# Attention decode layer, forward and backward: the products of a pair moved behind the next pair's maximum, and the depth of the K and V loads changed

## The chip, the cores and the metric

The kernel runs on one core of a Trainium2 chip. The metric is device time in microseconds (us) of one execution. Three runs of the kernel before took 1701.25, 1701.69 and 1703.4 us, a median of 1701.69 us.

## The reference

One layer for decoding, with its gradients: a layer norm, attention of one new token per batch entry over a cache of 4096 keys (4 batch entries, 32 heads, head size 128), a residual, a second layer norm, a SwiGLU block, and then the vector-Jacobian product with a given output gradient. There are 128 (batch, head) pairs, called heads below; K and V of one head are 1024 KB each in bf16. The reference, cut to what matters:

```python
q = (layernorm(x) @ wq).reshape(B, 1, H, Dh).transpose(0, 2, 1, 3)
scores = einsum("bhqd,bhkd->bhqk", q, k_cache) * Dh**-0.5
p = softmax(scores)                               # over 4096 keys
o = einsum("bhqk,bhkd->bhqd", p, v_cache)
h = x + o.transpose(0, 2, 1, 3).reshape(B, 1, H * Dh) @ wo
out = h + swiglu(layernorm(h), w1, w3, w2)
# outputs: out, and the gradients for grad_out of x, k_cache, v_cache, wq, wo, w1, w3, w2
```

The gradients of the two caches are 128 MB each, and they are written out in full. Every head's K is read once and its V twice, once in the forward part and once in the backward part.

## The kernel before

The forward part goes over the heads in 64 pairs. For a pair it transposes K, multiplies by the query (S), takes the softmax, and then forms for each head PK, the keys scaled by their probabilities, on VectorE (DVE). One run of matrix products of V with PK gives M for a head, a 128 x 128 matrix from which the backward part takes the gradient of the query without reading K again; a last column of it is the head's output. The iterations overlap: in iteration gi the pair a = 2 gi, a + 1 goes through the softmax, the next pair's K (na, nb) is transposed, and M of the heads m1 = a - 3 and m2 = a - 2 is made.

All large buffers are slots that hold one head (or as much of something else), 23 in all. A slot that is given back goes to the end of a queue of free slots, and a load takes the one at its head; the load then waits until the last reader of what lay in that slot is done. All loads are issued by one engine (SyncE, SP), in the order of the program. M of 16 heads takes one slot for good, so the slots in use by M grow from one to eight in the forward part.

The parts that matter, cut where marked by `...`:

```python
G, VQ, NSLOT, NPE = 2, 3, 23, 1      # heads in a pair, V heads ahead, slots, head chunks transposed on TensorE
# NH = 128 heads, NGI = 64 pairs, MC = 16 heads in one M slot, SJ = 32 key chunks of a head, Dh = P = 128

    free = deque(range(NSLOT))

    class Slot:
        def __init__(self, name, src=free):
            self.i = src.popleft()
            self.t = slotp.tile([P, SLOT], BF16, name=name, tag=f"slot{self.i}")

        ...
        def heads(self):
            return self.t[:, 0:SJ * Dh].rearrange("p (j d) -> p j d", d=Dh)

        def give(self):
            free.append(self.i)

    def load_K(s):
        if s < NH:
            Ks[s] = Slot("Kn")
            nc.sync.dma_start(out=Ks[s].heads(), in_=cache_head(A_k_cache, s))

    def load_V(s):
        if s < NH and s >= nvl["n"]:
            nvl["n"] = s + 1
            Vs[s] = Slot("Vn")
            nc.sync.dma_start(out=Vs[s].heads(), in_=cache_head(A_v_cache, s))

    def more_K(s):
        while len(Ks) + kdone["n"] < min(NH, s + 8) and len(free) > 1:
            load_K(len(Ks) + kdone["n"])

    def T_pe(s):
        KTs[s] = Slot("KT")
        KT, Kn = KTs[s].heads(), Ks[s].heads()
        for c in range(NPE):
            pt = psT.tile([P, GW, P], BF16, tag="tps", name="pt_tps")
            for i in range(GW):
                nc.tensor.transpose(pt[:, i, :], Kn[:, c * GW + i, :], ident_b[:])
            nc.scalar.copy(out=KT[:, c * GW:(c + 1) * GW, :], in_=pt[:])

    def T_dve(s, c, n=1):
        KT, Kn = KTs[s].b().bitcast(FP32), Ks[s].b().bitcast(FP32)
        w_ = GW * Dh // 2
        nc.vector.transpose(out=KT[:, c * w_:(c + n) * w_], in_=Kn[:, c * w_:(c + n) * w_])

    def q_stationaries(gi): ...     # GpSimd: the query columns of a pair, W and zq

    def S_head(gi, hl):             # TensorE: 16 score products of one head, then its KT slot is free
        ...
        KTs.pop(s).give()

    # softmax of a pair, one step each:
    # sm_max    DVE   mx <- S_ps (max over the free dim), mxm <- mx
    # sm_max_T  PE    x_ps <- transpose of mxm
    # sm_gmax   DVE   gm <- x_ps
    # sm_bcast  PE    b_ps <- gm
    # sm_exp    DVE   nm <- b_ps;  ACT  E <- exp(S_ps, nm), row sums
    # sm_sum    PE    l_ps <- row sums
    # sm_norm   DVE   rl <- l_ps;  ACT  Pn <- E, rl
    # sm_P      PE    pt_P <- 8 transposes of Pn;  ACT  P_all <- pt_P (4 copies)

    def PK_pairs(s):
        PKs[s] = Slot("PK")
        PK = PKs[s].t[:].rearrange("p (j c) -> p j c", c=PKW)
        nc.gpsimd.tensor_copy(out=PK[:, :, Dh:PKW], in_=P_all[:, s, :, None].to_broadcast([P, SJ, 2]))

    def PK_mul(s):
        PK = PKs[s].t[:].rearrange("p (j c) -> p j c", c=PKW)
        nc.vector.tensor_tensor(
            out=PK[:, :, 0:Dh].rearrange("p j (r t) -> p j r t", t=2),
            in0=Ks[s].heads().rearrange("p j (r t) -> p j r t", t=2),
            in1=PK[:, :, None, Dh:PKW].to_broadcast([P, SJ, Dh // 2, 2]),
            op=ALU.mult,
        )
        Ks.pop(s).give()
        kdone["n"] += 1

    def M_mm(s, j0, j1):
        if j0 == 0:
            hold["M"] = psM.tile([P, PKW], FP32, name="M_ps", tag="M")
        PK = PKs[s].t[:].rearrange("p (j c) -> p j c", c=PKW)
        Vn = Vs[s].heads()
        for j in range(j0, j1):
            nc.tensor.matmul(hold["M"][:], lhsT=Vn[:, j, :], rhs=PK[:, j, :], start=(j == 0), stop=(j == SJ - 1))

    def M_end(s):
        w = s % 32
        PK = PKs[s].t[:].rearrange("p (j c) -> p j c", c=PKW)
        if w == 0:
            hold["kP"] = psK.tile([P, 4, Dh], FP32, name="kP_ps", tag="kP")
        for c in range(2):
            for q in range(4):
                j0 = (c * 4 + q) * 4
                nc.tensor.matmul(hold["kP"][32 * q:32 * (q + 1), :, :], lhsT=ones_window(w), rhs=PK[:, j0:j0 + 4, 0:Dh],
                                 start=(w == 0 and c == 0), stop=(w == 31 and c == 1), tile_position=(0, 32 * q))
        if s % MC == 0:
            Ms.append(Slot("M"))
        nc.scalar.copy(out=M_of(s), in_=hold["M"][:, 0:Dh + 1])
        PKs.pop(s).give()
        Vs.pop(s).give()

    def kP_flush(s): ...            # once in 32 heads: the key sums, out of PSUM and onto columns (takes a slot and gives it back)
    def O_cols(s0, s1): ...         # once in 16 heads: two small DVE copies

    for gi in range(NGI):
        nxt = gi < NGI - 1
        a, na, nb = gi * G, gi * G + 2, gi * G + 3
        m1, m2 = a - 3, a - 2
        pk1 = a - 1
        has1, has2, hasp = 0 <= m1 < NH, 0 <= m2 < NH, 0 <= pk1 < NH
        S_head(gi, 0)
        S_head(gi, 1)
        weights(gi)
        if has1:
            M_mm(m1, 0, 16)
        sm_max(gi)
        if nxt:
            q_stationaries(gi + 1)
            T_pe(na)
            T_dve(na, 1)
        sm_max_T(gi)
        if has1:
            M_mm(m1, 16, SJ)
        sm_gmax(gi)
        sm_bcast(gi)
        if nxt:
            T_dve(na, 2)
        sm_exp(gi)
        if has1:
            M_end(m1)
            load_V(m1 + VQ)
            if m1 % 32 == 31:
                kP_flush(m1)
            if m1 % MC == MC - 1 and m1 < NH - 1:
                O_cols(m1 - MC + 1, m1 + 1)
        if hasp:
            PK_pairs(pk1)
        if nxt:
            T_dve(na, 3)
            T_pe(nb)
            T_dve(nb, 1)
        sm_sum(gi)
        sm_norm(gi)
        if gi == NGI - 1:

            nc.scalar.sqrt(warm[:], warm[:])
        if hasp:
            PK_mul(pk1)
            more_K(pk1 + 1)
        weights(gi)
        if has2:
            M_mm(m2, 0, 24)
        sm_P(gi)
        if has2:
            M_mm(m2, 24, SJ)
            M_end(m2)
            load_V(m2 + VQ)
        weights(gi)
        PK_pairs(a)
        if nxt:
            T_dve(nb, 2, 2)
        PK_mul(a)
        more_K(a + 1)
        weights(gi)
        hold.pop(gi - 3, None)
        if 2 <= gi:
            step("d")

    # after the loop: products and M of the last heads, the attention output, layer norm, the MLP forward and
    # its gradient, then the first output gradient (grad_V(0)); in this part wo, w1, w3 and nine heads of V are loaded ahead
    # backward, per head: V transposed on TensorE, dP, and on VectorE the outer products gv and gk, 1024 KB out each
    ...
```

Of the kernel before, what the change touches and what calls it, by code (L numbers as in the profile page):

```python
# [13 lines left out]
AX = mybir.AxisListType  # L14

G = 2
VQ = 3
SLOT = 4160
NSLOT = 23
JQ = 8  # L20
# [4 lines left out]
def kernel(  # L25
# [22 lines left out]
    nc = tc.nc  # L48
# [6 lines left out]
    Dh = A_k_cache.shape[3]  # L55
    F = B_w1.shape[1]
    NH = B * H
# [4 lines left out]
    SJ = Sk // P  # L62
# [4 lines left out]
    MC = 16  # L67
# [83 lines left out]


    def more_K(s):
        while len(Ks) + kdone["n"] < min(NH, s + 8) and len(free) > 1:
            load_K(len(Ks) + kdone["n"])

    kdone = {"n": 0}
# [152 lines left out]
    hold = {}  # L310
# [5 lines left out]
# [13 lines that stand above are left out]
# [29 lines left out]
    def sm_max(gi):  # L358
        st = hold[gi]
        mx = fw.tile([P, 1], FP32, tag="mx", name="mx")  # L360
        nc.vector.tensor_reduce(out=mx[:], in_=st["S"][:], axis=AX.X, op=ALU.max)
        st["mxm"] = fw.tile([P, G], FP32, tag="mxm", name="mxm")
        nc.vector.tensor_scalar(out=st["mxm"][:], in0=maskneg[:], scalar1=mx[:], scalar2=None, op0=ALU.add)

    def sm_max_T(gi):
        st = hold[gi]
        st["x"] = psX.tile([P, 512], FP32, tag="x", name="x_ps")
        nc.tensor.transpose(st["x"][0:G, 0:P], st["mxm"][:], ident_f[:])

    def sm_gmax(gi):  # L370
        st = hold[gi]
        st["gm"] = fw.tile([G, 1], FP32, tag="gm", name="gm")
        nc.vector.tensor_reduce(out=st["gm"][:], in_=st["x"][0:G, 0:P], axis=AX.X, op=ALU.max)

    def sm_bcast(gi):
        st = hold[gi]
        st["b"] = psX.tile([P, 512], FP32, tag="x", name="b_ps")
        nc.tensor.matmul(st["b"][:, 0:1], lhsT=selg[:], rhs=st["gm"][:], start=True, stop=True)

    def sm_exp(gi):  # L380
        st = hold[gi]
        nm = fw.tile([P, 1], FP32, tag="nm", name="nm")
        nc.vector.tensor_copy(out=nm[:], in_=st["b"][:, 0:1])  # L383
        st["E"] = fw.tile([P, JQ, 32], FP32, tag="E", name="E", bufs=1)
        st["rs"] = fw.tile([P, 1], FP32, tag="rs", name="rs")
        nc.scalar.activation(out=st["E"].rearrange("p j l -> p (j l)"), in_=st["S"][:], func=AF.Exp, bias=nm[:],  # L386
                             scale=scale, accum_out=st["rs"][:])
# [15 lines left out]
    def sm_P(gi):  # L403
        st = hold[gi]
        pt = psT.tile([P, JQ, P], BF16, tag="tps", name="pt_P")
        for jj in range(JQ):
            nc.tensor.transpose(pt[:, jj, :], st["Pn"][:, jj].rearrange("p q l -> p (q l)"), ident_b[:])  # L407
        v = pt.rearrange("p jj (c g q) -> p g c jj q", c=4, q=4)
        for q in range(4):
            r_ = slice(32 * q, 32 * (q + 1))  # L410
            nc.scalar.copy(out=P_all[r_, gi * G:(gi + 1) * G, :].rearrange("p g (c jj) -> p g c jj", c=4),  # L411
                           in_=v[r_, 0:G, :, :, q])
# [32 lines that stand above are left out]
                j0 = (c * 4 + q) * 4  # L445
                nc.tensor.matmul(hold["kP"][32 * q:32 * (q + 1), :, :], lhsT=ones_window(w), rhs=PK[:, j0:j0 + 4, 0:Dh],  # L446
                                 start=(w == 0 and c == 0), stop=(w == 31 and c == 1), tile_position=(0, 32 * q))
        if s % MC == 0:
            Ms.append(Slot("M"))
        nc.scalar.copy(out=M_of(s), in_=hold["M"][:, 0:Dh + 1])  # L450
        PKs.pop(s).give()
        Vs.pop(s).give()

    def kP_flush(s):
        ks = Slot("kP_sb")
        kP_sb = ks.f(4 * Dh).rearrange("p (c d) -> p c d", c=4)
        nc.scalar.copy(out=kP_sb, in_=hold["kP"][:])
        kt_ps = psM.tile([P, PKW], FP32, tag="M", name="kt_ps")
        for c in range(4):
            nc.tensor.matmul(kt_ps[:, 0:H], lhsT=kP_sb[:, c, :], rhs=sel_f[:], start=(c == 0), stop=(c == 3))  # L460
        nc.scalar.copy(out=kPT[:, s - 31:s + 1], in_=kt_ps[:, 0:H])
        ks.give()


    def O_cols(s0, s1):
        nc.vector.tensor_copy(out=OT_f[:, s0:s1], in_=Ms[s0 // MC].f(MC * (Dh + 1)).rearrange("p (n c) -> p n c", c=Dh + 1)[
            :, s0 % MC:s0 % MC + s1 - s0, Dh])
        nc.vector.tensor_copy(out=OT_bf[:, s0:s1], in_=OT_f[:, s0:s1])
# [123 lines left out]
    def weights(gi):  # L592
        if gi in reserve:
            while nvl["n"] < NH and len(free) > reserve[gi]:
                load_V(nvl["n"])
            pump(reserve[gi])
# [14 lines left out]

    for gi in range(NGI):
        nxt = gi < NGI - 1
        a, na, nb = gi * G, gi * G + 2, gi * G + 3
        m1, m2 = a - 3, a - 2
        pk1 = a - 1
        has1, has2, hasp = 0 <= m1 < NH, 0 <= m2 < NH, 0 <= pk1 < NH
        S_head(gi, 0)  # L620
        S_head(gi, 1)
        weights(gi)
        if has1:
            M_mm(m1, 0, 16)
        sm_max(gi)
        if nxt:
            q_stationaries(gi + 1)
            T_pe(na)
            T_dve(na, 1)
        sm_max_T(gi)  # L630
        if has1:
            M_mm(m1, 16, SJ)
        sm_gmax(gi)
        sm_bcast(gi)
        if nxt:
            T_dve(na, 2)
        sm_exp(gi)
        if has1:
            M_end(m1)
            load_V(m1 + VQ)  # L640
            if m1 % 32 == 31:
                kP_flush(m1)
            if m1 % MC == MC - 1 and m1 < NH - 1:
                O_cols(m1 - MC + 1, m1 + 1)
        if hasp:
            PK_pairs(pk1)
        if nxt:
            T_dve(na, 3)
            T_pe(nb)
            T_dve(nb, 1)  # L650
        sm_sum(gi)
        sm_norm(gi)
        if gi == NGI - 1:

            nc.scalar.sqrt(warm[:], warm[:])
        if hasp:
            PK_mul(pk1)
            more_K(pk1 + 1)
        weights(gi)
        if has2:  # L660
            M_mm(m2, 0, 24)
        sm_P(gi)
        if has2:
            M_mm(m2, 24, SJ)
            M_end(m2)
            load_V(m2 + VQ)
        weights(gi)
        PK_pairs(a)
        if nxt:
            T_dve(nb, 2, 2)  # L670
        PK_mul(a)
        more_K(a + 1)
        weights(gi)
        hold.pop(gi - 3, None)
        if 2 <= gi:
            step("d")

    c1b.close()
    c1b = ExitStack()
    psT = c1b.enter_context(tc.tile_pool(name="psTm", bufs=4, space=bass.MemoryType.PSUM))  # L680
# [21 lines left out]
    O_cols(NH - MC, NH)  # L702
    attn_page(2)
    attn_page(3)
    kP_flush(NH - 1)
    weights(NGI)
    assert not pending
    c1b.close()
# [594 lines left out]
```

## Time and profile before

The profile is of one execution, with a span of 1700.1 us. Its parts, from the table of busy time by stretches (the borders are chosen by the reader of the profile; TensorE's clock was 0.99 to 1.00 of full speed from 40 to 660 us):

| stretch (us) | what runs | DVE busy (us) | PE busy (us) | GB/s moved |
|---|---|---|---|---|
| 0 to 40 | start | 21.68 | 21.35 | 399 |
| 40 to 440 | forward | 369.27 | 346.66 | 424 |
| 440 to 600 | forward | 146.99 | 133.22 | 418 |
| 600 to 660 | last forward pairs | 54.37 | 49.30 | 407 |
| 660 to 740 | end of forward, middle, start of backward | 50.64 | 66.66 | 388 |
| 740 to 1660 | backward | 587.25 | 625.22 | 423 |

The profile moved 707.50 MB in all. Over the whole span DVE was busy 73 per cent, PE 73, ACT (ScalarE) 57 and POOL (GpSimd) 24 per cent.

How to read it: PE is TensorE, and SPq is the issue of transfers by SyncE. A row of a timeline gives start and duration in us, the engine, the line of the program, the operation with output and inputs by their names, and in brackets how long the engine had been idle and which instruction ended that wait. A row of the table of waits gives who waited, for whom, the sum in us, how many times, and the longest. In a kernel that is limited by its transfers, an engine's idle time costs only where it lets the transfer engines run dry.

### The profile page before, as it was taken

To read this page: it belongs to the slowest core of one execution; us is meant where nothing else is said; L and a number is where in the kernel's file an instruction comes from. 1 tells how busy PE (TensorE), PEld (TensorE's weight loads), DVE (VectorE), ACT (ScalarE), POOL (GpSimd) and SP (SyncE) were. 2 spreads that over 40 slices of the span, in tenths; PEclk is the share of its full clock that TensorE was granted. 3 is DMA by queue.
4 is the path that set the end of the run, shared out by engine and by line. 5 is a ranking of instruction groups with operands and counts; after the bars stand their busy time and mean duration, and the time that the engine had idled before them with its cause. 6 is when DMAs were issued, how large, how long until landed. Compare 5 with 4: busy or idle time off the path is not lost.

```text
span 1700.1 us, 38407 instructions
## 1 busy us (share of the span) xinstructions
PE 1242.4 (73%) x16180; PEld 915.5 (54%) x16180; DVE 1236.5 (73%) x1294; ACT 968.9 (57%) x1502; POOL 406.4 (24%) x678
## 2 busy tenths in 40 slices
PE   5889888888888888877877664786676566586550
PEld 4777676666666666655655443443444343344330
DVE  5989999999998997667776665674557466566672
ACT  3555444544454444677766564676677566576550
POOL 1211222222222231324352111142112222210120
PEclk8999999999999999799899897977799778777775
DMA  9999999999999999999999999999999999999996
GB/s 401 424 424 424 424 424 424 424 423 424 417 422 412 423 405 400 385 415 425 425 424 426 425 426 426 425 426 426 425 423 420 419 423 417 423 420 414 416 423 275
DMA packets 101741, 707.50 MB, mean 416 GB/s; under 512 B 11052, under 2 KB 15288, under 8 KB 17600
## 3 DMA queue, kind: packets, MB, share of 16 engines
q1 hardware_dynamic: 101152, 704.95, 99.4%
q8 instruction: 127, 2.08, 0.5%
q14 instruction: 46, 0.38, 0.1%
q0 software_dynamic: 416, 0.10, 0.0%
HBM read 422.59 MB, written 282.34 MB: 415 GB/s over the span
## 4 chain that ended last, share of the span: by engine, by line
DMA 37%; ACT 10%; PE 7%; issue 1%; DVE 1%; DVEq 0%; SPq 0%; ACTq 0%; POOL 0%
DMA out_dram<-gv 14%; DMA out_dram<-gk 12%; DMA V<-in_A_v_cache_dram 9%; ACT V L765 9%; PE pt_tps L764 2%; PE dq_ps L962 2%; PE dP_ps L1182 2%; DMA out_dram<-gwo 1%; DVE gk L770 1%; DVE gv L770 1%; PE rep_ps L1133 0%; ACT dPr L1157 0%; PE pt_wo L574 0%; ACT reps L1136 0%; PE o_ps L1059 0%
## 5 line engine op out<-in xcount | busy, mean ns | idle before, releaser
L765 ACT COPY V<-pt_tps 128x1024 bf16<-128x1024 bf16 x512 | 490.2, 1024 | 132.9 <-PE pt_tps L764 128.5
L764 PE MATMUL pt_tps<-ident_b,V 128*128 128x128 bf16 x4096 | 353.3, 247 | 192.4 <-ACT V L765 152.9
L764 PEld LDWEIGHTS <-V 128*128 128x128 bf16 x4096 | 303.1, 113 | 264.0 <-issue 199.0
L770 DVE TENSOR_TENSOR gv<-P,reps 128x4096 bf16<-128x4096 bf16 x125 | 286.3, 2293 | 191.3 <-DMA out_dram<-gv 100.3
L770 DVE TENSOR_TENSOR gk<-dS,reps 128x4096 bf16<-128x4096 bf16 x128 | 293.1, 2292 | 103.8 <-DMA out_dram<-gv 89.8
L421 DVE TENSOR_TENSOR PK<-Kn,PK 128x4096 bf16<-128x4096 bf16 x128 | 292.3, 2284 | 26.1 <-POOL PK L417 25.7
L436 PE MATMUL M_ps<-PK,Vn 128*128 128x130 bf16 x4096 | 284.3, 221 | 32.8 <-DMA Vn<-in_A_v_cache_dram 32.0
L436 PEld LDWEIGHTS <-Vn 128*128 128x128 bf16 x4096 | 252.0, 99 | 53.2 <-DMA Vn<-in_A_v_cache_dram 45.5
L328 DVE STREAM_TRANSPOSE KT<-Kn 128x512 f32<-128x512 f32 (+1 forms) x321 | 250.6, 797 | 0.3 <-issue 0.2
L323 ACT COPY KT<-pt_tps 128x1024 bf16<-128x1024 bf16 x128 | 129.5, 1012 | 186.4 <-PE pt_tps L322 153.0
L1182 PE MATMUL dP_ps<-V,zd 128*32 128x512 bf16 x1024 | 181.2, 431 | 68.0 <-ACT V L765 64.6
L1152 POOL COPY P<-P_all 128x64 bf16<-128x64 bf16 x125 | 100.5, 806 | 447.3 <-DVE gv L770 440.0
L1147 POOL COPY zd<-dOT_bf 128x2 bf16<-128x2 bf16 x128 | 131.4, 1028 | 155.3 <-PE dP_ps L1182 155.2
L334 POOL TENSOR_TENSOR W<-qrep,wmask 128x128 bf16<-128x128 bf16 x128 | 123.8, 967 | 82.4 <-PE S_ps L354 67.6
L417 POOL COPY PK<-P_all 128x64 bf16<-128x64 bf16 x128 | 32.6, 254 | 414.3 <-ACT P_all L411 411.3
L1182 PEld LDWEIGHTS <-zd 128*32 128x32 bf16 x1024 | 37.7, 95 | 156.5 <-issue 141.8
L411 ACT COPY P_all<-pt_P 32x64 bf16<-32x64 bf16 x256 | 52.1, 203 | 53.1 <-PE pt_P L407 50.8
L322 PE MATMUL pt_tps<-ident_b,Kn 128*128 128x128 bf16 x1024 | 80.4, 223 | 0.0
L446 PE MATMUL kP_ps<-PK,onesw 128*32 128x512 bf16 x1024 | 79.1, 386 | 0.0
L386 ACT ACTIVATE E<-S_ps,nm 128x256 f32<-128x256 f32 x64 | 30.4, 474 | 80.4 <-DVE nm L383 80.4
L322 PEld LDWEIGHTS <-Kn 128*128 128x128 bf16 x1024 | 62.0, 100 | 25.8 <-issue 25.8
L354 PE MATMUL S_ps<-KT,W 128*32 128x256 bf16 x1536 | 75.3, 285 | 0.5 <-DVE KT L328 0.2
(239 smaller groups left out, 1226.0 us busy)
## 6 DMA issues: line engine op xcount, KB each, us to landing
Kn<-in_A_k_cache_dram SPq DMA_DIRECT2D x128, 1024.0 KB, 15.4
Vn<-in_A_v_cache_dram SPq DMA_DIRECT2D x128, 1024.0 KB, 15.6
V<-in_A_v_cache_dram SPq DMA_DIRECT2D x128, 1024.0 KB, 19.9
out_dram<-gv SPq DMA_DIRECT2D x128, 1024.0 KB, 20.0
out_dram<-gk SPq DMA_DIRECT2D x128, 1024.0 KB, 20.1
wq<-in_A_wq_dram SPq DMA_DIRECT2D x8, 1024.0 KB, 15.5
out_dram<-gw SPq DMA_DIRECT2D x6, 896.0 KB, 19.8
wo<-in_A_wo_dram SPq DMA_DIRECT2D x4, 1024.0 KB, 11.7
```

The costliest lines, as they stand in the source:

```text
L322: nc.tensor.transpose(pt[:, i, :], Kn[:, c * GW + i, :], ident_b[:])
L323: nc.scalar.copy(out=KT[:, c * GW:(c + 1) * GW, :], in_=pt[:])
L328: nc.vector.transpose(out=KT[:, c * w_:(c + n) * w_], in_=Kn[:, c * w_:(c + n) * w_])
L334: nc.gpsimd.tensor_tensor(out=W[:, hl], in0=qrep[:, :, s:s + 1].to_broadcast([P, 4, 32]), in1=wmask[:, hl, None, :].to_broadcast([P, 4, 32 ...
L421: nc.vector.tensor_tensor(out=PK[:, :, 0:Dh].rearrange("p j (r t) -> p j r t", t=2), in0=Ks[s].heads().rearrange("p j (r t) -> p j r t", t=2),
L436: nc.tensor.matmul(hold["M"][:], lhsT=Vn[:, j, :], rhs=PK[:, j, :], start=(j == 0), stop=(j == SJ - 1))
L764: nc.tensor.transpose(pt[:, i, :], v[:, g * GW + i, :], ident_b[:])
L765: nc.scalar.copy(out=v[:, g * GW:(g + 1) * GW, :], in_=pt[:])
L770: nc.vector.tensor_tensor(out=dst.rearrange("p j (r t) -> p j r t", t=2), in0=col2[:, :, None, :].to_broadcast([P, SJ, Dh // 2, 2]), in1=r ...
L1147: nc.gpsimd.tensor_copy(out=zd[s % B][:, 32:132:67], in_=dOT_bf[:, s:s + 1].to_broadcast([P, 2]))
L1152: nc.gpsimd.tensor_copy(out=P2s[s][:], in_=P_all[:, s, :, None].to_broadcast([P, SJ, 2]))
L1182: nc.tensor.matmul(rows["acc"][32 * c:32 * (c + 1), :], lhsT=zq_window(zd[hl], 2 * hl + u), rhs=VT[:, j0:j0 + 4, :], start=(hl == 0 and u ...
```

## The change

The order of the forward loop is changed, and with it the depth of two load queues.

- The product PK of the pair's first head (m2 = a - 2) is moved from the end of an iteration to the next one, behind the next pair's maximum (sm_max). The product of the second head (a - 1) is moved from the middle of an iteration to its end. The maximum of the next pair so leads the product on DVE, and the product lies beside the transpose of the maximum on TensorE.
- The transposes of both heads of the next pair on TensorE (T_pe) come at the start of the iteration, T_pe(nb) ahead of the transpose of the maximum. Those on DVE (T_dve) are spread over the steps of the softmax.
- The end of M (M_end), which gives back a PK slot and a V slot, comes earlier in the iteration for both heads. M of the second head starts ahead of the sum of the softmax.
- kP_flush is split in two parts, so that its products do not follow its copy at once.
- V is loaded five heads ahead of the head whose M is done (before: three), and K seven heads ahead of the head whose product was just formed (before: eight).

The purpose is to take the waits within the softmax of a pair out of DVE's path, by putting a product into them.

The diff, its core:

```diff
--- before.py
+++ after.py
@@ -14,7 +14,7 @@
 AX = mybir.AxisListType
 
 G = 2
-VQ = 3
+VQ = 5
 SLOT = 4160
 NSLOT = 23
 JQ = 8
@@ -151,7 +151,7 @@
 
 
     def more_K(s):
-        while len(Ks) + kdone["n"] < min(NH, s + 8) and len(free) > 1:
+        while len(Ks) + kdone["n"] < min(NH, s + 7) and len(free) > 1:
             load_K(len(Ks) + kdone["n"])
 
     kdone = {"n": 0}
@@ -445,22 +445,25 @@
                 j0 = (c * 4 + q) * 4
                 nc.tensor.matmul(hold["kP"][32 * q:32 * (q + 1), :, :], lhsT=ones_window(w), rhs=PK[:, j0:j0 + 4, 0:Dh],
                                  start=(w == 0 and c == 0), stop=(w == 31 and c == 1), tile_position=(0, 32 * q))
+        PKs.pop(s).give()
+        Vs.pop(s).give()
         if s % MC == 0:
             Ms.append(Slot("M"))
         nc.scalar.copy(out=M_of(s), in_=hold["M"][:, 0:Dh + 1])
-        PKs.pop(s).give()
-        Vs.pop(s).give()
-
-    def kP_flush(s):
-        ks = Slot("kP_sb")
+
+    def kP_copy():
+        hold["ks"] = Slot("kP_sb")
+        kP_sb = hold["ks"].f(4 * Dh).rearrange("p (c d) -> p c d", c=4)
+        nc.scalar.copy(out=kP_sb, in_=hold["kP"][:])
+
+    def kP_columns(s):
+        ks = hold.pop("ks")
         kP_sb = ks.f(4 * Dh).rearrange("p (c d) -> p c d", c=4)
-        nc.scalar.copy(out=kP_sb, in_=hold["kP"][:])
         kt_ps = psM.tile([P, PKW], FP32, tag="M", name="kt_ps")
         for c in range(4):
             nc.tensor.matmul(kt_ps[:, 0:H], lhsT=kP_sb[:, c, :], rhs=sel_f[:], start=(c == 0), stop=(c == 3))
         nc.scalar.copy(out=kPT[:, s - 31:s + 1], in_=kt_ps[:, 0:H])
         ks.give()
-
 
     def O_cols(s0, s1):
         nc.vector.tensor_copy(out=OT_f[:, s0:s1], in_=Ms[s0 // MC].f(MC * (Dh + 1)).rearrange("p (n c) -> p n c", c=Dh + 1)[
@@ -611,70 +614,77 @@
 
 
 
+    def O_cols_of(m):
+        if m % MC == MC - 1 and m < NH - 1:
+            O_cols(m - MC + 1, m + 1)
+
+    def PK(s):
+        PK_mul(s)
+        more_K(s + 1)
+
     for gi in range(NGI):
         nxt = gi < NGI - 1
         a, na, nb = gi * G, gi * G + 2, gi * G + 3
         m1, m2 = a - 3, a - 2
-        pk1 = a - 1
-        has1, has2, hasp = 0 <= m1 < NH, 0 <= m2 < NH, 0 <= pk1 < NH
+        has1, has2 = m1 >= 0, m2 >= 0
         S_head(gi, 0)
         S_head(gi, 1)
         weights(gi)
-        if has1:
-            M_mm(m1, 0, 16)
-        sm_max(gi)
         if nxt:
             q_stationaries(gi + 1)
             T_pe(na)
+        sm_max(gi)
+        if has2:
+            PK(m2)
+        if has1:
+            M_mm(m1, 0, 16)
+        if nxt:
+            T_pe(nb)
+        sm_max_T(gi)
+        sm_gmax(gi)
+        if nxt:
             T_dve(na, 1)
-        sm_max_T(gi)
         if has1:
             M_mm(m1, 16, SJ)
-        sm_gmax(gi)
-        sm_bcast(gi)
-        if nxt:
-            T_dve(na, 2)
-        sm_exp(gi)
-        if has1:
             M_end(m1)
             load_V(m1 + VQ)
             if m1 % 32 == 31:
-                kP_flush(m1)
-            if m1 % MC == MC - 1 and m1 < NH - 1:
-                O_cols(m1 - MC + 1, m1 + 1)
-        if hasp:
-            PK_pairs(pk1)
+                kP_copy()
+        sm_bcast(gi)
+        weights(gi)
+        sm_exp(gi)
         if nxt:
+            T_dve(na, 2)
             T_dve(na, 3)
-            T_pe(nb)
-            T_dve(nb, 1)
+        if has2:
+            PK_pairs(a - 1)
+            M_mm(m2, 0, 16)
         sm_sum(gi)
         sm_norm(gi)
         if gi == NGI - 1:
 
             nc.scalar.sqrt(warm[:], warm[:])
-        if hasp:
-            PK_mul(pk1)
-            more_K(pk1 + 1)
-        weights(gi)
+        if has1:
+            O_cols_of(m1)
+        if nxt:
+            T_dve(nb, 1)
+            T_dve(nb, 2, 2)
         if has2:
-            M_mm(m2, 0, 24)
-        sm_P(gi)
-        if has2:
-            M_mm(m2, 24, SJ)
+            M_mm(m2, 16, SJ)
             M_end(m2)
             load_V(m2 + VQ)
+            PK(a - 1)
         weights(gi)
+        if has1 and m1 % 32 == 31:
+            kP_columns(m1)
+        sm_P(gi)
         PK_pairs(a)
-        if nxt:
-            T_dve(nb, 2, 2)
-        PK_mul(a)
-        more_K(a + 1)
         weights(gi)
         hold.pop(gi - 3, None)
         if 2 <= gi:
             step("d")
 
+    PK(NH - 2)
     c1b.close()
     c1b = ExitStack()
     psT = c1b.enter_context(tc.tile_pool(name="psTm", bufs=4, space=bass.MemoryType.PSUM))
@@ -702,7 +712,8 @@
     O_cols(NH - MC, NH)
     attn_page(2)
     attn_page(3)
-    kP_flush(NH - 1)
+    kP_copy()
+    kP_columns(NH - 1)
     weights(NGI)
     assert not pending
     c1b.close()
```

## The prediction

> **What bounds the kernel now.** I read the page first, for what moves at the full rate and where it doesn't.
>
> ```profile
> DMA  9999999999999999999999999999999999999996
> GB/s 401 424 424 424 424 424 424 424 423 424 417 422 412 423 405 400 385 415 425 425 424 426 425 426 426 425 426 426 425 423 420 419 423 417 423 420 414 416 423 275
> HBM read 422.59 MB, written 282.34 MB: 415 GB/s over the span
> ```
>
> The second row is the one to read: 40 slices of 42.5 us. The transfers run at 424 to 426 GB/s wherever nothing hinders them, so 707.5 MB need 707.5 / 0.4245 = 1667 us, and 33 us of the 1700 are lost. No order of the forward part can win more than that. About half of the 33 lies at the very end (last slice: 42.5 x (1 - 275/424.5) = 15 us), out of reach. The forward part ends near slice 16. From the table of stretches, 440 to 600 us loses 160 x (1 - 418/424.5) = 2.5 us, 600 to 660 loses 2.5, and 660 to 740 loses 80 x (1 - 388/424.5) = 6.9.
>
> Next the waits of TensorE for V, first in the stretch 40 to 440 us and then in 520 to 600 (total us, times, longest):
>
> ```profile
> PE M_ps L436 <- DMA Vn<-in_A_v_cache_dram: 21.0, 35, 1.8
> ```
>
> ```profile
> PE M_ps L436 <- DMA Vn<-in_A_v_cache_dram: 0.2, 1, 0.2
> ```
>
> Early, the engines wait for data. Late, they don't, and the timeline of DVE shows what they do instead; one iteration, pair 54:
>
> ```profile
> 566.64 0.42 DVE L361 TENSOR_REDUCE mx<-S_ps 128x1 f32<-128x256 f32 x1
> 567.09 0.41 DVE L363 TENSOR_SCALAR mxm<-maskneg,mx 128x2 f32<-128x2 f32 x1
> 567.41 0.70 DVE L328 STREAM_TRANSPOSE KT<-Kn 128x512 f32<-128x512 f32 x1
> 568.04 0.24 DVE L373 TENSOR_REDUCE gm<-x_ps 2x1 f32<-2x128 f32 x1
> 568.21 0.69 DVE L328 STREAM_TRANSPOSE KT<-Kn 128x512 f32<-128x512 f32 x1
> 569.11 0.16 DVE L383 COPY nm<-b_ps 128x1 f32<-128x1 f32 x1 [0.21 <-PE b_ps L378]
> 569.18 1.29 DVE L328 STREAM_TRANSPOSE KT<-Kn 128x512 f32<-128x512 f32 x2
> 570.67 0.17 DVE L397 RECIPROCAL rl<-l_ps 128x1 f32<-128x1 f32 x1 [0.20 <-PE l_ps L392]
> 570.76 2.29 DVE L421 TENSOR_TENSOR PK<-Kn,PK 128x4096 bf16<-128x4096 bf16 x1
> 572.96 1.24 DVE L328 STREAM_TRANSPOSE KT<-Kn 128x1024 f32<-128x1024 f32 x1
> 574.42 2.29 DVE L421 TENSOR_TENSOR PK<-Kn,PK 128x4096 bf16<-128x4096 bf16 x1 [0.22 <-POOL PK L417]
> ```
>
> From 526.64 the maximum (mx) starts every 10.0 us, while the four heads of a pair (2 of K, 2 of V, 4.194 MB) take 4.194/0.424 = 9.89 us. So late in the forward part DVE's chain is the bound by 0.1 us a pair, with 0.63 us of waits in it (the three brackets). Maxima stand at 607.18 (pair 58) and 657.20 (pair 63).
>
> Last the issues of SP after the forward loads:
>
> ```profile
> 653.35 9.77 SPq L550 DMA_DIRECT2D wo<-in_A_wo_dram  x4
> 663.22 5.21 SPq L544 DMA_DIRECT2D w<-in_B_w_dram  x4
> 668.52 27.69 SPq L797 DMA_DIRECT2D V<-in_A_v_cache_dram  x9
> 700.91 16.66 SPq L781 DMA_DIRECT2D out_dram<-gv  x7
> ```
>
> What can be loaded ahead is loaded by 696 us, because slots run out; then the transfers wait for the first gv, at the end of a chain through the last pair, the layer norm and the MLP. What is moved before and after the first gv does not depend on the order of the forward loop. So the **time shifts one for one with the first gv**, and that with the last pair's softmax.
>
> **What the Trainium skill says.** "VectorE: DVE Perf Modes", the perf-mode tier table: a two-tensor product in bf16 runs at twice the base rate, 1224 ns for 2048 elements. Twice that less one fixed part is an estimate of about 2.29 us for 4096; the trace has 2.28, so moving the product can't change its size. "DMA: Bandwidth & Descriptors", where 436 GB/s comes from: a ceiling of 435 for the fabric; the trace's 424 is at it. The same page, anatomy of one DMA: about 2 us fixed and then bytes at 436 GB/s, an estimate of 4.4 us for one head, and waits for semaphores happen at the issuing sequencer, not in the transfer engines. The trace's first wq load, alone, landed in 4.8 us, the four in a row within 11.3.
>
> **The change, part by part.**
>
> *Work.* Nothing is added or removed: still two products, six chunk transposes and the softmax per pair.
>
> *DVE's chain, new order.* Steps from start to start, taken from the timeline above: mx 0.45, mxm 0.32, product 2.2, gm 0.2, transpose 0.65, nm 0.07, two transposes 1.29, rl 0.09, transpose 0.65, two 1.24, product 2.2, together 9.36. Waits: on TensorE, after the maximum, 16 M products 1.0, T_pe(nb) 0.5, transpose of the maximum 0.3, 16 products 1.0, M_end 0.6, then b_ps and 0.48 to nm, that is 3.9 against DVE's 3.82: 0.1. From nm to rl by the old distance (1.56) against 1.36 of work: 0.2. PK's wait for POOL goes. Sum **9.6 to 9.7 us**, below the 9.89 of the transfers. So up to pair 58 the transfers stay at 424. Before pair 58, 236 heads have to have landed, plus wq, w2 and instruction fetches, about 254 MB: 40 us at 399, the rest at 424 gives 602 to 603 us against 607.2: **4 us won**.
>
> *Slots, late.* At the second K load of an iteration (K needs a spare slot left, so 22 of 23 may be taken) the program holds, before: M, 3 of V, 2 of PK, 2 of KT, so K gets 22 - 7 - M = 15 - M. With M at 8 (from pair 57) that is 7, and K reaches head 2 gi + 7, which is needed two iterations later. After: 5 of V, 1 of PK, 2 of KT, so K gets 14 - M: 7 while M has 7 slots, **6 from pair 57 on**. K then reaches only head 2 gi + 5, and that is nb of the very next iteration. Its slot is the V slot that M_end(m2) gives back. By the TensorE sums above M_end(m2) ends about 6.9 us after a maximum, T_pe(nb) comes 1.1 us after the next: a lead of 9.7 + 1.1 - 6.9 = 4 us. A V load is issued from the same release just ahead of it, so with empty queues K lands 4.8 + 2.5 = 7.3 us later. And T_pe(nb) now stands before the transpose of the maximum and before M_end(m1), in TensorE's order, so a late K stops everything, the release of further slots too.
>
> *The cost of that.* It hits pairs 59, 60, 61 and 62 (heads 121, 123, 125, 127). At pair 58 some two loads are still queued, K of 121 lands about 16 us after that maximum and is needed at 11: 5 us. Afterwards one iteration is T_pe(nb) to M_end(m2) 5.8, plus 7.4 to the landing: 13.2 us. T_pe(nb) at 604.1, then 619.0, 632.2, 645.4, 658.6; the maximum of pair 63 8.4 later, 667.0, against 657.2: **9.8 us lost**. In pair 63 gm stands behind the product of head 124, 3.85 us from mx to nm instead of 2.3: another 1.6. Net about +11, with 1 or 2 us of slack that I may not see: **+8 to +11.5**, of which the 4 won are already taken off.
>
> *V five ahead* puts V's load 2.5 iterations before its use, so the early waits of the M products for V go; but there the transfers are the bound, so that pays nothing, and the waiting moves to K.
>
> **The rivals.** (1) *Clean gain*: K of the next iteration comes in time after all. For it speaks that in the trace before loads land 11 us after issue only because others are ahead of them, and that V is far ahead by then. Then pair 63 comes at 603 + 5 x 9.7 = 651.5, with the tail +1.6: 1701.7 - 4 = 1697 to 1698. Against it speaks the count of slots. (2) *Hidden*: the order changes but the first gv hangs on the weights wo, w1, w3, whose loads come last; 1700 to 1703. Against it, the loads of w are issued by 668 us and the first gv comes 32 us later. (3) *DVE's chain gets longer*, because more TensorE work stands between the maximum and nm. If the iteration takes 10.0 to 10.1, 50 pairs lose 0.1 to 0.2 each from the start, 5 to 10 us, with the end on top of it: 1715 or more.
>
> **Range and chances.** The K wait at 0.68, with 1707 to 1714; clean gain 0.17, near 1697; hidden 0.1, near 1701; longer chain 0.05. The middle of this is 1709, and 1696.5 to 1716 holds it 8 times in 10. Two per cent is 34 us: more than all the losses of the profile, and three times what I expect to be lost.
>
> **What would show it.** Right, step by step: maxima 9.9 us apart until pair 58 and at about 603 there; 424 GB/s through 440 to 600; on DVE no bracket of PK behind POOL; then T_pe of heads 121 to 127 waiting for the load of K, four waits of 3 to 5 us, maxima 13 us apart, and a dip of the transfers between 610 and 665; the first gv near 709. Wrong: maxima below 10 us apart through pairs 59 to 62 (the slot count or the landing time is off), or about 10.0 all the way from pair 5 on (rival 3), or a first gv that doesn't move with pair 63 (rival 2). A changed rate in the backward part, which the change doesn't touch but for a later start, would also make it wrong.

## The result and the profile after

The changed kernel takes 1727.91 us (median of 4 runs, 1726.37 to 1729.18) against 1702.55 for the kernel before in the same comparison: a ratio of 1.0148, with a 95 per cent interval from 1.0131 to 1.0166. It is 25 us slower. The forecast had the direction and the place right and the size wrong: 1709, with a range that ended at 1716.

The page of the changed kernel, the two rows of transfers in 40 slices (now of 43.2 us), and the row of the TensorE transposes of K:

```profile
DMA  9999999999999978899999999999999999999996
GB/s 402 425 424 424 423 423 425 424 419 417 421 419 407 424 311 296 358 404 425 425 425 426 425 425 426 425 425 426 423 421 421 418 419 415 420 417 418 416 418 279
...
L322 PE MATMUL pt_tps<-ident_b,Kn 128*128 128x128 bf16 x1024 | 83.5, 228 | 80.0 <-DMA Kn<-in_A_k_cache_dram 79.8
```

The slices of the forward and backward parts look as before. Three slices, from about 605 to 735 us, fall to 311, 296 and 358 GB/s, where the kernel before had 405, 400 and 385. And TensorE's transposes of K, which had no idle time in front of them before, now have 80 us, all of it waiting for loads of K. Their row in the page of the kernel before:

```profile
L322 PE MATMUL pt_tps<-ident_b,Kn 128*128 128x128 bf16 x1024 | 80.4, 223 | 0.0
```

Of these 80 us, 57.5 us lie in the stretch 40 to 600 us, in small pieces, and 20.1 in the stretch 606 to 685, in large ones. The table of waits has them as (total, times, longest):

```profile
PE pt_tps L322 <- DMA Kn<-in_A_k_cache_dram: 57.5, 89, 3.3
```

```profile
PE pt_tps L322 <- DMA Kn<-in_A_k_cache_dram: 20.1, 7, 5.9
```

The larger sum also stands in kernels that are no slower than the one before, as the experiments show; the smaller one is the loss. The timeline of TensorE in pair 59 shows one of the large ones (the second row is the transpose of head 121; the score products are left out):

```profile
617.80 0.62 PE L322 MATMUL pt_tps<-ident_b,Kn 128*128 128x128 bf16 x8 [0.45 <-DMA Kn<-in_A_k_cache_dram]
...
625.36 1.03 PE L322 MATMUL pt_tps<-ident_b,Kn 128*128 128x128 bf16 x8 [5.90 <-DMA Kn<-in_A_k_cache_dram]
626.19 0.42 PE L368 MATMUL x_ps<-ident_f,mxm 128*2 128x128 f32 x1
626.40 1.94 PE L436 MATMUL M_ps<-PK,Vn 128*128 128x130 bf16 x16
628.27 1.04 PE L446 MATMUL kP_ps<-PK,onesw 128*32 128x512 bf16 x8
```

TensorE stands 5.90 us, and behind it, in its order, the transpose of the maximum, M of head m1 and M_end. DVE in the same pair waits twice, first for that transpose and then for b_ps:

```profile
618.24 0.41 DVE L361 TENSOR_REDUCE mx<-S_ps 128x1 f32<-128x256 f32 x1
...
618.82 2.29 DVE L421 TENSOR_TENSOR PK<-Kn,PK 128x4096 bf16<-128x4096 bf16 x1
...
626.65 0.28 DVE L373 TENSOR_REDUCE gm<-x_ps 2x1 f32<-2x128 f32 x1 [5.54 <-PE x_ps L368]
...
629.87 0.16 DVE L383 COPY nm<-b_ps 128x1 f32<-128x1 f32 x1 [2.32 <-PE b_ps L378]
...
635.25 0.42 DVE L361 TENSOR_REDUCE mx<-S_ps 128x1 f32<-128x256 f32 x1
```

The second wait I had not foreseen. The same stretch in narrow windows (window, length, then busy us and instructions of PE, PEld, DVE, ACT and POOL, TensorE's granted clock, the transfers' share, GB/s) explains it:

```profile
620.00:622.00 2.00, 0.00 (x0) 0.00 (x0) 1.11 (x1) 0.00 (x0) 2.00 (x4) 1.00 1.02 422
622.00:624.00 2.00, 0.00 (x0) 0.00 (x0) 0.00 (x0) 0.00 (x0) 0.00 (x0) 0.81 1.01 418
624.00:625.00 1.00, 0.00 (x0) 0.00 (x0) 0.00 (x0) 0.00 (x0) 0.00 (x0) 0.50 0.97 410
627.00:628.00 1.00, 1.00 (x12) 1.00 (x10) 0.55 (x1) 0.45 (x1) 0.00 (x0) 0.50 0.04 16
629.00:630.00 1.00, 1.00 (x9) 0.74 (x6) 0.13 (x2) 0.00 (x0) 0.00 (x0) 0.50 0.00 0
630.00:631.00 1.00, 1.00 (x18) 1.00 (x16) 1.00 (x3) 0.57 (x2) 0.00 (x0) 0.96 0.68 106
```

While TensorE waits, its clock is halved, and it stays at half until 630 us. So the 16 products of M take 1.94 us instead of 1.10. And read the last column: while the slow TensorE works off the steps that release the next slots, the transfers come to a stand, at 16 and then 0 GB/s. Everything waits for a slot.

The maxima of pairs 58 to 63 stand at 608.87, 618.24, 635.25, 649.81, 666.32 and 680.60 us, up to 17 us apart. The first gv is issued here:

```profile
726.72 16.16 SPq L792 DMA_DIRECT2D out_dram<-gv  x7
```

That is 25.8 us later than before, and the program ends 25.4 us later (medians): what the first gv loses, the end loses.

### The profile page after: what moved, and what is told of

Read it like the earlier page. It is cut to its first block, busy times and chain, and to the rows that moved or that the text cites. A ratio compares the mean times of both kernels' runs of the same rounds, so it can differ in the third digit from the quotient of the medians.

```text
span 1727.3 us, 38444 instructions
## 1 busy us (share of the span) xinstructions
PE 1266.5 (73%) x16180; PEld 916.7 (53%) x16180; DVE 1222.4 (71%) x1294; ACT 974.2 (56%) x1502; POOL 495.6 (29%) x678
## 4 chain that ended last, share of the span: by engine, by line
DMA 50%; ACT 2%; PE 1%; DVE 1%; issue 0%; DVEq 0%; SPq 0%; ACTq 0%; POOL 0%
DMA out_dram<-gv 20%; DMA out_dram<-gk 14%; DMA V<-in_A_v_cache_dram 13%; ACT V L776 1%; DMA out_dram<-gwo 1%; DMA out_dram<-gw 1%; DMA wq<-in_A_wq_dram 1%; PE pt_tps L775 1%; DVE gv L781 1%; DVE gk L781 1%; PE dP_ps L1193 0%; PE gps L957 0%; ACT dPr L1168 0%; DVEq L1309 0%; PE rep_ps L1144 0%
## 5 line engine op out<-in xcount | busy, mean ns | idle before, releaser
L775 PEld LDWEIGHTS <-V 128*128 128x128 bf16 x4096 | 299.5, 112 | 267.0 <-issue 201.7
L436 PEld LDWEIGHTS <-Vn 128*128 128x128 bf16 x4096 | 259.1, 100 | 18.2 <-issue 10.9
L328 DVE STREAM_TRANSPOSE KT<-Kn 128x512 f32<-128x512 f32 (+1 forms) x321 | 244.0, 791 | 0.2 <-issue 0.2
L1163 POOL COPY P<-P_all 128x64 bf16<-128x64 bf16 x125 | 94.6, 758 | 446.1 <-DVE gv L781 446.0
L417 POOL COPY PK<-P_all 128x64 bf16<-128x64 bf16 x128 | 74.0, 578 | 402.2 <-ACT P_all L411 267.7
L1158 POOL COPY zd<-dOT_bf 128x2 bf16<-128x2 bf16 x128 | 126.5, 989 | 168.8 <-PE dP_ps L1193 168.6
L334 POOL TENSOR_TENSOR W<-qrep,wmask 128x128 bf16<-128x128 bf16 x128 | 153.3, 1197 | 19.7 <-DVE qrep L286 14.5
L400 ACT ACTIVATE Pn<-E,rl 128x1024 bf16<-128x1024 f32 x64 | 73.7, 1151 | 49.5 <-DVE rl L397 44.4
## 6 DMA issues: line engine op xcount, KB each, us to landing
out_dram<-gk SPq DMA_DIRECT2D x128, 1024.0 KB, 20.1
```

The costliest lines, as they stand in the source:

```text
L334: nc.gpsimd.tensor_tensor(out=W[:, hl], in0=qrep[:, :, s:s + 1].to_broadcast([P, 4, 32]), in1=wmask[:, hl, None, :].to_broadcast([P, 4, 32 ...
L775: nc.tensor.transpose(pt[:, i, :], v[:, g * GW + i, :], ident_b[:])
L1158: nc.gpsimd.tensor_copy(out=zd[s % B][:, 32:132:67], in_=dOT_bf[:, s:s + 1].to_broadcast([P, 2]))
L1163: nc.gpsimd.tensor_copy(out=P2s[s][:], in_=P_all[:, s, :, None].to_broadcast([P, SJ, 2]))
```

## The experiments

Two theories stood against each other. A: *the depths*. V five heads ahead takes a slot that K needs once M holds eight, K then comes only one iteration ahead of its use, and pairs 59 to 62 pay for it. B: *the order*. A transpose that waits for K ahead of the transpose of the maximum makes the softmax slow, whatever the depths. A result is given as median us, and the ratio to the kernel before on the same chip with its interval. The kernel before had medians of 1702.1 to 1703.1 us in these comparisons, so that differences below 1 us between rows are to be read from the ratios. All experiments in one table, with the maxima of pairs 58 and 63 and the issue of the first gv from their profiles:

| kernel | us | ratio, 95% interval | pair 58 | pair 63 | first gv |
|---|---|---|---|---|---|
| before (old order, V 3, K 8) | 1702.55 | | 607.18 | 657.20 | 700.91 |
| changed (new order, V 5, K 7) | 1727.91 | 1.0148 (1.0131 to 1.0166) | 608.87 | 680.60 | 726.72 |
| new order, V 4, K 7 | 1702.12 | 0.9995 (0.9986 to 1.0004) | 607.86 | 655.38 | 700.17 |
| new order, V 4, K 8 | 1702.46 | 1.0000 (0.9991 to 1.0008) | 604.66 | 655.20 | 701.49 |
| new order, V 3, K 8 | 1701.88 | 0.9994 (0.9985 to 1.0002) | 606.15 | 654.33 | 699.49 |
| old order, V 5, K 7 | 1714.91 | 1.0070 (1.0055 to 1.0085) | 610.09 | 668.25 | 713.16 |
| new order, V 4, K 7, a slot less | 1724.60 | 1.0124 (1.0107 to 1.0141) | 606.16 | 679.00 | 725.00 |
| changed, TensorE kept busy | 1722.59 | 1.0114 (1.0099 to 1.0129) | 607.48 | 674.09 | 720.28 |
| changed, T_pe(nb) late | 1711.43 | 1.0048 (1.0033 to 1.0063) | 611.32 | 663.79 | 709.22 |
| new order, T_pe(nb) late, V 4, K 8 | 1702.40 | 0.9996 (0.9987 to 1.0004) | 604.18 | 654.88 | 700.21 |
| before, a slot less | 1705.30 | 1.0017 (1.0010 to 1.0024) | 609.06 | 659.08 | 702.79 |
| new order, V 3, K 8, a slot less | 1700.66 | 0.9989 (0.9982 to 0.9995) | 605.76 | 652.38 | 698.31 |
| new order, V 3, K 8, last pair changed | 1706.30 | 1.0022 (1.0012 to 1.0031) | 606.10 | 654.71 | 703.49 |
| new order, V 3, K 7 | 1703.54 | 1.0007 (0.9999 to 1.0015) | 605.08 | 657.74 | 702.02 |

### The order and the depths, apart

The changed kernel with V four ahead:

```diff
-VQ = 5
+VQ = 4
```

> The changed kernel with V loaded four heads ahead instead of five, K seven as it is. Theory A (K slots: five V heads leave K one slot too few once M holds eight): K keeps 15 - M = 7 slots, reaches head 2 gi + 6 up to the last pairs, the waits of 4 to 6 us at pairs 59 to 62 go, and most of the 25 us with them: 1700 to 1706. Theory B (the new order itself is slow, since a TensorE transpose that waits for K now stands ahead of the transpose of the maximum): the time stays above 1720.

Measured: 1702.12. That is theory A's number, and B is out: the order is the same. The waits of TensorE for K, first in the stretch 40 to 600 us and then in 606 to 680:

```profile
PE pt_tps L322 <- DMA Kn<-in_A_k_cache_dram: 55.8, 88, 3.2
```

```profile
PE pt_tps L322 <- DMA Kn<-in_A_k_cache_dram: 2.7, 5, 0.7
```

The early sum is as in the changed kernel (57.5), and yet the time is that of the kernel before; the late one has gone from 20.1 to 2.7, and the 25 us with it.

With K eight ahead as well:

```diff
-VQ = 5
+VQ = 4
-        while len(Ks) + kdone["n"] < min(NH, s + 7) and len(free) > 1:
+        while len(Ks) + kdone["n"] < min(NH, s + 8) and len(free) > 1:
```

> The changed kernel with V four and K eight heads ahead. Theory A: K reaches 2 gi + 7 up to pair 56 and 2 gi + 6 after; the short waits of TensorE for K in the stretch 40 to 600 us (57.5 us in the changed kernel) shrink to under 20, and the time is 1697 to 1702, a little below the kernel with V four and K seven. Theory B: above 1720, as the order is the same.

Measured: 1702.46. The time is as expected, but the early waits for K only fell to 39.4 us, not below 20. They are the waits of a loop that is limited by its transfers, and they appear wherever the loop asks first.

The new order with the old depths:

```diff
-VQ = 5
+VQ = 3
-        while len(Ks) + kdone["n"] < min(NH, s + 7) and len(free) > 1:
+        while len(Ks) + kdone["n"] < min(NH, s + 8) and len(free) > 1:
```

> The new order with the old depths, V three and K eight heads ahead: the order alone. Theory A: K reaches 2 gi + 7 to the end, so no wait for K at the end; V is loaded only 1 to 1.3 iterations (10 to 13 us) before its use, so TensorE waits for V instead, which costs little where the transfers are the bound: 1698 to 1706. Theory B: the order alone brings most of the loss, above 1718.

Measured: 1701.88. TensorE now waits for V (47.6 us in the stretch 40 to 600) and hardly for K; the time is that of the kernel before. The order alone is worth nothing measurable.

The kernel before with the new depths:

```diff
-VQ = 3
+VQ = 5
-        while len(Ks) + kdone["n"] < min(NH, s + 8) and len(free) > 1:
+        while len(Ks) + kdone["n"] < min(NH, s + 7) and len(free) > 1:
```

> The old order with the new depths, V five and K seven heads ahead: the depths alone. Here two PK slots are held, K has 13 - M slots and reaches only head 2 gi + 5 from pair 57 on, as in the changed kernel. Theory A: waits for K at pairs 59 to 62, 1710 to 1725; a little less than the changed kernel, as the transpose of the second head stands later in TensorE's order. Theory B: the old order hides it, 1700 to 1705.

Measured: 1714.91, theory A again. The depths alone cost 12 us in the old order and 26 in the new one (against V 3, K 8 in each). So the order is no cause by itself, but it doubles what the depths cost.

### Is it the slots?

V's depth could hurt in another way: its loads stand ahead of K's in one queue. This kernel keeps V at four and takes a slot away, by holding one that nobody uses:

```diff
+    spare = Slot("spare")
     for gi in range(NGI):
+        if gi == NGI - 2:
+            spare.give()
```

> The kernel with V four and K seven heads ahead in the new order (1702.1 us), with one slot taken and left unused through pairs 0 to 61. The V depth and the order stay, only the count of slots falls by one, and K reaches head 2 gi + 5 from pair 57 on, as in the changed kernel. If the slot count is the cause: waits of TensorE for K of 3 to 6 us at pairs 59 to 61 and 1716 to 1726. If V's depth of five costs in another way (more V loads ahead of K in the queue), the time stays near 1702 to 1706.

Measured: 1724.60, all but 3 to 4 us of the loss. TensorE's late waits for K (606 to 680 us) are back, with no V load more than in the fast kernel:

```profile
PE pt_tps L322 <- DMA Kn<-in_A_k_cache_dram: 20.6, 6, 6.4
```

So it is the count of slots, and V's fifth head is only what used the last one up. Whether any slot less would do that was asked twice, with the same edit in the kernel before and in the new order with V three and K eight. In both, K still reaches head 2 gi + 6 at the end.

> The kernel before (old order, V three, K eight) with one slot taken and left unused through pairs 0 to 61. K then gets 14 - M slots and reaches head 2 gi + 6 from pair 57 on, still one full iteration before its use. If what matters is that K must not fall to head 2 gi + 5: within 3 us of the kernel before. If any slot less costs, because the late forward part lives on the number of loads in flight: 1706 to 1715.

> The new order with V three and K eight heads ahead and one slot left unused. K reaches head 2 gi + 6 from pair 57 on. If only a fall to 2 gi + 5 hurts: 1700 to 1704, as with all slots (1701.9), and not 22 us more as with V four and K seven. If any slot less costs: 1706 or more.

Measured: 1705.30, which is 2.8 us slower, and 1700.66, which is 1.9 us faster than the kernel before. So a slot less costs little or nothing by itself, and the step of 22 us belongs to the point at which K falls from head 2 gi + 6 to 2 gi + 5. The second of these is the one version whose interval lies below 1, by 0.05 to 0.18 per cent; it is not told apart from the same version with all its slots, whose interval (0.9985 to 1.0002) overlaps with it. Its DVE timeline in pair 60 has no wait that the profile marks, one maximum to the next 9.22 us:

```profile
624.33 0.42 DVE L361 TENSOR_REDUCE mx<-S_ps 128x1 f32<-128x256 f32 x1
...
625.06 2.28 DVE L421 TENSOR_TENSOR PK<-Kn,PK 128x4096 bf16<-128x4096 bf16 x1
627.26 0.27 DVE L373 TENSOR_REDUCE gm<-x_ps 2x1 f32<-2x128 f32 x1
...
628.09 0.11 DVE L383 COPY nm<-b_ps 128x1 f32<-128x1 f32 x1
...
629.54 0.17 DVE L397 RECIPROCAL rl<-l_ps 128x1 f32<-128x1 f32 x1
...
633.55 0.41 DVE L361 TENSOR_REDUCE mx<-S_ps 128x1 f32<-128x256 f32 x1
```

This is what the new order was made for, and with it DVE's chain is 0.8 us shorter a pair than the old one's 10.0. It shows only in the last pairs, in which the loads are ahead.

### Why the same shortage costs more in the new order

In the changed kernel T_pe(nb) stands ahead of both M_end. Moved behind them:

```diff
-        if nxt:
-            T_pe(nb)
         sm_max_T(gi)
 ...
-        if nxt:
-            T_dve(nb, 1)
-            T_dve(nb, 2, 2)
         if has2:
             M_mm(m2, 16, SJ)
             M_end(m2)
             load_V(m2 + VQ)
+        if nxt:
+            T_pe(nb)
+            T_dve(nb, 1)
+            T_dve(nb, 2, 2)
+        if has2:
             PK(a - 1)
```

> The changed kernel with its depths, but the TensorE transpose of the second head (and the two DVE transposes after it) moved behind M_end of both heads and the V load. A late K then no longer holds up the release of the slots that the next K needs, and its lead grows from 4 to about 10 us. If the place of the transpose makes the wait so dear: 1700 to 1708. If only the slot count matters: above 1718.

Measured: 1711.43, between the two expectations. The maxima of pairs 59 to 62 are 10.45 us apart now, not 14 to 17, and TensorE's late waits for K are down to 0.2 us: the place of the transpose carried most of the loss. The 10.45 contain a new wait, of DVE, here in pair 60:

```profile
638.75 1.84 DVE L328 STREAM_TRANSPOSE KT<-Kn 128x512 f32<-128x512 f32 x2 [1.36 <-PE kP_ps L446]
```

The KT slot of the second head is now taken behind M_end(m2), and it is the slot that M_end(m2) gives back. DVE waits 1.36 us in each iteration for it, and 1.36 on top of the 9.1 that are left of the chain is the 10.45. Whether this wait is the rest of the loss shows in the same late transpose with V four and K eight:

> The same late transpose with V four and K eight heads ahead: no shortage of K slots and no K wait ahead of the maximum. If the new order can pay at all, this shows it: waits for K in the stretch 40 to 600 us under 10 us in sum, and 1696 to 1700. If the transfers take all of it back: 1701 to 1703, equal to the kernel before.

Measured: 1702.40. It has the same wait of DVE, and maxima 10.45 us apart, without being slower than the kernel before:

```profile
642.07 1.84 DVE L328 STREAM_TRANSPOSE KT<-Kn 128x512 f32<-128x512 f32 x2 [1.36 <-PE kP_ps L446]
```

So the wait alone does not explain the 8.7 us that the other one loses. Of the 9.0 us between their first gv, 7.1 are there at pair 58 already (611.32 against 604.18), before the last pairs: with the late transpose, the greater part of what V five and K seven still cost arises earlier in the forward part. Why was not followed.

The early waits for K fell to 1.3 us, as expected, and TensorE waited 45.1 us for V instead; with the transpose early and the same depths it had been 39.4 for K and 1.2 for V. The time did not move. This is the clearest case of the early waits changing their name.

### The halved clock

Fourteen products that nobody reads keep TensorE busy for part of its wait in pairs 59 to 62 (they are extra work; the outputs do not use them):

```diff
+        if 59 <= gi <= 62:
+            fill = psX.tile([P, 512], FP32, tag="x", name="fill_ps")
+            for _ in range(14):
+                nc.tensor.matmul(fill[:], lhsT=ident_b[:], rhs=qrep.rearrange("p a n -> p (a n)"), start=True, stop=True)
         if nxt:
             T_pe(nb)
```

> The changed kernel with 14 products of 512 columns that nobody reads, put on TensorE just ahead of the transpose of the second head in pairs 59 to 62, inside its wait for K. In the changed kernel the granted clock falls to 0.50 during that wait and stays there for about 4 us after it. If that slow stretch is what made an iteration 15 us and not the forecast 13.2, the wait of nm for b_ps falls from 1.8 to 2.3 us to below 0.5 in these pairs and the time falls by 4 to 7 us, to 1721 to 1724. If the clock costs nothing, the time stays at 1728 or rises by what the filler delays, up to 2 us.

Measured: 1722.59, which is 5 to 6 us less than the changed kernel; the time is as expected. TensorE's timeline in pair 59:

```profile
619.14 3.18 PE L644 MATMUL fill_ps<-qrep,ident_b 128*128 128x512 bf16 x14
625.03 0.62 PE L322 MATMUL pt_tps<-ident_b,Kn 128*128 128x128 bf16 x8 [2.71 <-DMA Kn<-in_A_k_cache_dram]
625.49 0.27 PE L368 MATMUL x_ps<-ident_f,mxm 128*2 128x128 f32 x1
625.60 1.10 PE L436 MATMUL M_ps<-PK,Vn 128*128 128x130 bf16 x16
```

K lands at the same time as before (625.03 against 625.36), but behind it the 16 products take 1.10 us and not 1.94. From T_pe(nb) to the end of M_end(m2) it takes 5.3 us in pairs 59 to 61, as in pair 58 of the changed kernel, and not 6.8 to 7.3. DVE's wait for b_ps fell from 2.3 and 1.9 us to 0.90 in pairs 59 to 61, not to below 0.5 as expected. In pair 62 the clock fell to 0.50 in spite of the filler, after 2.0 us of idleness behind it, and the wait for b_ps was still 1.93. From pair 58 to 63 it took 66.6 us in place of 71.7. Useless work made the kernel faster by 0.3 per cent.

### The last pair, and the last try

The way from the last maximum to the first gv is 43.7 us before and 46.1 in the changed kernel. To shorten it, the product of head 124 was moved behind rl in the last pair only:

```diff
         sm_max(gi)
-        if has2:
+        if has2 and nxt:
             PK(m2)
 ...
-            M_mm(m2, 0, 16)
+            if nxt:
+                M_mm(m2, 0, 16)
         sm_sum(gi)
         sm_norm(gi)
+        if not nxt:
+            PK(m2)
+            M_mm(m2, 0, 16)
```

> The new order with V three and K eight heads ahead, and in the last pair the product of head 124 moved from between the maximum and gm to behind rl, where DVE waits anyway. In the changed kernel the way from the last maximum to the first gv is 46.1 us, in the kernel before 43.7. If the product in the last pair's softmax is what makes it longer, about 1 us comes back and the time is 1700 to 1701.5, 0.1 per cent below the kernel before; if not, it stays at 1701.9.

Measured: 1706.30, a miss: between 4 and 5 us slower than without the edit. DVE's timeline in the last pair says why:

```profile
659.32 4.49 DVE L421 TENSOR_TENSOR PK<-Kn,PK 128x4096 bf16<-128x4096 bf16 x2
667.45 2.29 DVE L421 TENSOR_TENSOR PK<-Kn,PK 128x4096 bf16<-128x4096 bf16 x1 [3.65 <-POOL PK L417]
```

M of head 124 needs the moved product, and on TensorE it stands ahead of the transposes of the last probabilities, so these came late, and through them the product of head 126. I had looked at DVE's order alone. Nor was there 1 us to win: from the maximum to nm it takes 3.2 us with the edit and 3.6 without.

The last run asked whether a K load less in flight was what made the version with a slot less the fastest:

```diff
-VQ = 5
+VQ = 3
```

> The new order with V three and K seven heads ahead, all slots in use: K reaches head 2 gi + 6 throughout, as it did at the end in the kernel with one slot left unused (1700.7 us), and V's loads stand earlier in the queue than with K eight ahead. If that balance is what made the kernel with fewer slots the fastest: maxima of pairs 58 to 62 about 9.3 us apart and 1700 to 1701.5. If the engines wait for K and V in turn because 10 heads ahead are too few to keep the transfers full: below 422 GB/s in the stretch 40 to 440 us and 1703 or more.

Measured: 1703.54, a miss, though not a clear loss. The maxima of pairs 58 to 62 are 9.0 to 10.0 us apart as hoped, but from pair 62 to 63 it takes 15.0 us, with one wait for K of 3.4 us. The transfers ran at 410 to 467 GB/s through that wait, and at 424 in the stretch 40 to 440, so that they were kept full, against the second expectation. Why the wait arises here was not followed, and so it stays open what, if anything, the version with a slot less gains from the slot.

## Why the prediction was wrong in size and right in kind

*Right.* The bound, the shift of the end with the first gv, the count of slots, the heads and pairs concerned, the first wait (5 us forecast, 5.9 measured), the 1.6 us in the last pair (2.4 measured). Of the rivals, the hidden one is out, since the first gv moved by 25.8 us; the clean gain is out for these depths. The longer chain is out as well: DVE's new chain is 9.2 us where nothing disturbs it, shorter than the 9.6 to 9.7 of my sum.

*Wrong.* What failed is the size of the loss in the part "The cost of that": it gave +11.4 us at the first gv, and +25.8 was measured. The mechanism stands: the K load that comes one iteration ahead of its use, and the TensorE order in which its wait holds up the next release. The missing 14.4 lie in three terms.

1. *Pair 58: 4.2 us won, 1.7 lost; 5.9 us.* I let the transfers stay at 424 GB/s up to pair 58. In the stretch 440 to 600 us they ran at 417, against 418 before, and at 417 to 421 in the versions with V four ahead and in the new order with the old depths. A shorter chain on DVE hardly lifted the rate; what I took for DVE's bound in the late forward part, 10.0 us a pair, was near the rate of the loads anyway. That the free slots set this rate is only supported (the kernel before with a slot less falls to 414 there and loses 2.8 us), not isolated. And the rate is the smaller part: 160 us at 417 in place of 424 lose 2.6 us. The rates of the stretches give an estimate of what had been moved at the maximum of pair 58 (40 us at 400, 400 at 423, 169 at 418): about 256 MB and not 254, which is some 4 us more. The sum had an error too, since 254 MB at its own rates come to 601.4 us and not to 602 or 603.
2. *Pairs 58 to 63: 14.0 us more than before forecast, 21.7 measured; 7.7 us.* The term that failed most is "T_pe(nb) to M_end(m2) 5.8". It took 7.3, 6.8 and 7.2 us in pairs 59, 60 and 61, because TensorE's clock was halved by the wait itself; at full clock it took 5.3, in pair 58 and with the filler. The filler gives back 5.1 us of this stretch. Most of the rest is the landing of K, 7.8, 9.3 and 7.6 us behind M_end(m2) and not 7.4; what made the second of them longer was not followed. The Trainium skill would have told the first of these: "TensorE: Matmul & The Clock Gate", on the HAM clock gate, says that the array falls to half its rate after an idle window of about 3.4 us and needs about as long under work to come back. The trace agrees with it in the main: in the four waits the clock fell after 2.9 to 3.8 us of idleness and came back 3.1 to 4.7 us after work began. The 2.9 us, and the 2.0 us in pair 62 of the filler version, are shorter than the page's window; there the measurement decides. I had the page at hand and forecast waits of 3 to 5 us without asking what they do to the clock.
3. *The last pair: 1.6 forecast, 2.4 measured; 0.8 us.* From the maximum to nm it took 3.6 us instead of 2.3, which is 1.3 of the 1.6; where the other 1.1 us lie was not followed.

And one error is not of mechanics: I had reckoned the wait at 8 to 11.5 us, each term with no margin upwards, and then drawn the middle down to 1709 for the chance of a clean gain. Where a late load delays the release that the next load needs, a term that is taken too small is paid again in each of the four pairs, so the range ought to have been open above.

## What to carry to other kernels

Where loads take their buffers from one shared pool, a deeper queue for one stream is a shallower one for another; count, for the moment at which most of the pool is taken, which load comes last and how far it is from its use. A load whose buffer is released only an iteration before its use must not stand, in an engine's order, ahead of the work that releases the next buffer, or each wait sets up the next. And where TensorE waits for a transfer, add the slow clock behind the wait to the estimate: here waits of 3.8 to 5.9 us made the 5.3 us of work behind them 1.4 to 2.0 us longer.

## What the runs showed of the hardware

- TensorE's granted clock fell from 1.00 to 0.50 after 2.9 to 3.8 us of idleness in the four long waits of the changed kernel, and rose again 3.1 to 4.7 us after work began. The length of the wait alone does not tell when: read from narrow windows, the clock changed at 623.26, 630.08, 640.32, 643.74, 653.98, 660.80, 671.04 and 674.46 us, each time one, two or three times 3.41 us after the change before; the changes in the version with V four, K seven and a slot less lie on such steps too. With 3.2 us of useless products inside each wait it fell in one pair of four only, there after 2.0 us of idleness; in another it did not fall in 2.7.
- Waiting for loads is not a loss by itself. In the new order with V four and K seven, 55.8 us of TensorE's waits for K in the stretch 40 to 600 us went with a time equal to that of the kernel before. With V four and K eight, moving the transpose turned 39.4 us of waits for K into 1.3, and 1.2 us of waits for V into 45.1, at 1702.46 and 1702.40 us.
